# A fused memory-attention and mixture-of-experts kernel: splits of the first steps kept behind the prologue, some remainders on GpSimd, the last two token tiles one by one

## The chip, the cores and the metric

The kernel runs on one core of one Trainium2 chip. The metric is the device time of one execution in microseconds (us). The kernel before takes 1411.16 us, the median of three runs that lie between 1411.07 and 1411.36 us.

## The reference: what is computed

There are 8 batches with 8 heads, 576 tokens, head dimension 64, and 32 memory slots for each head. First comes an attention through the memory:

```python
a = softmax(phi, axis=2)                        # phi: (8, 8, 576, 32)
k_m = einsum('bhsm,bhsd->bhmd', a, k)           # 32 memory keys per head
v_m = einsum('bhsm,bhsd->bhmd', a, v)           # 32 memory values per head
attn = softmax(q @ k_m.T / sqrt(64))            # (8, 8, 576, 32)
x = (attn @ v_m) -> (4608 tokens, 512)
p = domain_probs / domain_probs.sum(-1)         # 4 experts
out = sum over e of p[:, e] * (relu(x @ w1[e]) @ w2[e])   # w1: 512x1024, w2: 1024x512
```

All of it is in 32-bit floats.

## The kernel before

**Two-part numbers.** TensorE multiplies in a rounded 32-bit form. To keep the precision, most operands are split in two: ScalarE casts the value to the rounded form (the high part), and another engine subtracts that from the value (the low part, here called the remainder). A product then takes three matmuls: high by high, high by low and low by high. `split` (L146 to L148) does this for weights: the cast is L147, the subtraction L148, on VectorE (DVE) or GpSimd (POOL) as its caller says.

**The work.** x is never formed. v_m is multiplied with w1 first (`vw_mm`, L458 to L463, and its two parts `vw_out`, L480 and L482), so that the first layer of an expert is one product of the transposed attention weights AT with that table vw. Two batches make a pair of 1152 tokens, nine token tiles of 128. A pair has 4 experts with 32 steps each (`first` and `second`); a step is one of the 8 blocks of 128 hidden units (j) for one half of one batch's tokens. `first(s)` makes h, the x product and its relu (matmuls L553 to L555, ScalarE L565, VectorE's remainder L567); `second(s)` multiplies two or three token tiles of h with w2 (L583 to L585) and sums over j in PSUM. `first` runs two steps ahead of `second`. When a half ends, `accumulate` (L603, L605) adds the probability-weighted sum into acc and, at the last expert, stores 256 KB per token tile from SyncE's queue (L607).

**Order.** The beginning (batch 0 up to the first two `first`) and everything from step 36 on stand in a `manual_schedule`: each engine runs them in the written order. Steps 0 to 35 are placed by the library's scheduler, which may move their instructions ahead, also into the gaps of the prologue. What a step does besides `first` and `second` is in a plan. Step 1 has, in this order: the scores of the last token group of batch 0, the splits of w1 for fh 1 (the upper half of the hidden units; four tiles), the splits of w2 for j = 2 to 5, v_m x w1 for hp 0 and 2 with fh 1, and batch 1's phi chain. Step 2 has the scores of the next token group and v_m x w1 for hp 1 and 3; step 5 has w2 for j = 6 and 7. Batch 1's keys and values follow at steps 6 to 10 (`unit_kv`, remainders on GpSimd, three buffers for the split parts), its v_m at 11. At steps 16 and 22 `v_split` casts v_m of batches 0 and 1 into two parts (vh), which two steps later are written to vs by 8 small DMAs for each batch. `phi_max` of batch 1 is already kept in program order.

**The prologue's middle.** For batch 0 the written order is: scores, `scores_max` (L401, L404), the split of w1 hp 1, the v_m tables of group 1 (`write_vt_0`, ScalarE L353 and VectorE L354), two further w1 splits with remainders on GpSimd, v_m x w1, `scores_exp` (L410), `vw_out` for hp 0, `soft` (L417 to L420), `vw_out` for hp 1 and 2, `transposes` (L441) and their copies AT (L452, L453), `vw_out` for hp 3, two w2 splits with remainders on GpSimd, `first(0)`, `first(1)`. `keep_warm` puts in products whose result isn't used.

**Loads.** All loads and stores go through SyncE's queue, in its order. Weights, keys and queries share four staging buffers of 512 KB; a load waits until the splits that read its buffer are done. The order of these loads is the order of the plan.

Of the kernel before, what the change touches and what calls it, by code (L numbers as in the profile page):

```python
# [40 lines left out]
N, DM, E, F = 4608, 512, 4, 1024  # L41
P = 128
# [4 lines left out]
NJ = F // P  # L47
TP = 2 * S // P
# [3 lines left out]
LAST = NG * PAIR  # L52
# [39 lines left out]
def body(ctx: ExitStack, tc: tile.TileContext, qm, qt, kv, kvt, phi, prob, w1, w1d, w2, out):  # L92
    nc = tc.nc
# [3 lines left out]
    psum = pool("psum", space=PSUM)  # L97
# [7 lines left out]
    pt = const.tile([P, N // P, E], F32, name="pt")  # L105
# [37 lines left out]

    w1t, w2t = {}, {}

    def split(dst, raw, eng):  # L146
        nc.scalar.copy(dst[:, 0, :], raw)  # L147
        eng.tensor_sub(dst[:, 1, :], raw, dst[:, 0, :].bitcast(F32))  # L148

    def split_w1(raw, fh, hp, eng):  # L150
        t = wp.tile([P, 2, 512], F32R, name="w1", tag="w1", bufs=4)
        split(t, raw[:, hp % 2, :], eng)
        w1t[fh, hp] = t

    def unit_w1(k, e, fh, g):
        def emit(raw):
            for i in range(2):
                split_w1(raw, fh, 2 * g + i, nc.vector)
        return ("w1", e, fh, g), emit

    def split_w2(k, e, j, raw, eng=nc.vector):
        t = wp.tile([P, 2, DM], F32R, name="w2", tag="w2", bufs=NJ + 1)
        split(t, raw[:, j % 2, :], eng)
        w2t[k, e, j] = t

    def units_w1(e, fh, g):
# [20 lines left out]
    st = {}  # L187
# [153 lines left out]
    def slot(b, h):  # L341
        return h ^ TURN[b % 4]

    def write_vt_0(b, gs=slice(0, 2)):

        vt = vts[b // 2].rearrange("p (g a) s c -> p g a s c", g=2)
        v = st["v", b].rearrange("p (g a) m -> p g a m", g=2)
        for h in range(4):
            q = slot(b, h)
            r = slice(64 * (h % 2), 64 * (h % 2) + 64)  # L350
            dst = vt[r, gs, h // 2, :, M * q:M * q + M]
            x = v[r, gs, q // 2, :]
            nc.scalar.copy(dst[:, :, 0, :], x)  # L353
            nc.vector.tensor_sub(dst[:, :, 1, :], x, dst[:, :, 0, :].bitcast(F32))  # L354

    def v_split(b):

        st["vh", b] = att.tile([P, 2, NP, M], F32R, name="vh", tag="vh")
        split(st["vh", b].rearrange("p s a m -> p s (a m)"),
              st["v", b].rearrange("p a m -> p (a m)"), nc.gpsimd)  # L360

    def write_v(b, pair):

# [170 lines left out]
    hs, mid, acc, po, ended = {}, {}, {}, {}, []  # L534

    def where(s):
        k, s = divmod(s, PAIR)
        e, s = divmod(s, STEPS)
        odd, s = divmod(s, 2 * NJ)
        half, j = divmod(s, NJ)  # L540
        return k, e, odd, half, j

    def first(s):
# [25 lines left out]
            )  # L569
        hs[s] = h  # L570

    def second(s):
        k, e, odd, half, j = where(s)
        h = hs.pop(s)
        w = w2t[k, e, j]
        t0 = (0, 2, 5, 7)[2 * odd + half]
        left = [(t0 + i, h[:, :, i * P:i * P + P]) for i in range(2)]
        if t0 == 5:
            left.append((4, mid[j]))
        for t, x in left:  # L580
            if j == 0:
                po[t] = psum.tile([P, DM], F32, name="p2", tag="p2", bufs=4)
            nc.tensor.matmul(po[t], x[:, 0, :], w[:, 0, :], start=j == 0, stop=False)  # L583
            nc.tensor.matmul(po[t], x[:, 0, :], w[:, 1, :], start=False, stop=False)  # L584
            nc.tensor.matmul(po[t], x[:, 1, :], w[:, 0, :], start=False, stop=j == NJ - 1)  # L585
        if j == NJ - 1:
            ended.append((k, e, t0, [t for t, _ in left]))

    def accumulate():
        if not ended:  # L590
            return
        k, e, t0, left = ended.pop()
        if e == 0:
            a = work.tile([P, 1024], F32, name="acc", tag="acc", bufs=4)
            for i in range(2):
                acc[k, t0 + i] = a[:, i * DM:i * DM + DM]
            if t0 == 5:
                acc[k, 4] = work.tile([P, DM], F32, name="accm", tag="accm", bufs=1)
        for t in left:
            a, n = acc[k, t], TP * k + t  # L600
            p = pt[:, n, e:e + 1]
            if e == 0:
                nc.vector.tensor_scalar_mul(a, po[t], p)  # L603
            else:
                nc.vector.scalar_tensor_tensor(a, po[t], p, a, ALU.mult, ALU.add)  # L605
            if e == E - 1:
                nc.sync.dma_start(out[n * P:n * P + P, :], a)  # L607


    plan = defaultdict(list)  # L610
# [15 lines left out]

    rest = [unit_scores(0, t0) for t0 in (2, 4)]
    rest += [lambda t0=t0: (transposes(0, t0), transposes_out(0, t0)) for t0 in (2, 4)]
    rest += [unit_w1(0, 0, 1, g) for g in range(2)]
    rest += [unit_w2(0, 0, j2) for j2 in range(1, 4)]  # L630
    rest += [lambda hp=hp: vw_unit(0, 0, 1, hp, (0,), ("pm", 4)) for hp in range(NP)]
    for s, u in zip(REST_0, rest):
        at(s, u)
# [120 lines left out]
    with tc.manual_schedule():  # L754
        raw = {key: take(later) for later, key in enumerate(early)}
        stage_ahead(len(early) + 4)
        nc.scalar.copy(att.tile([P, 1], F32, name="woken", tag="woken"), ident[:, :1])
        nc.sync.dma_start(pt, prob)
        keep_warm(10)
        dve, gps = nc.vector, nc.gpsimd  # L760
        for g in range(2):
            phi_max(0, g)
        for g in range(2):
            phi_exp(0, g)
        kvr = lambda hp: raw["kv", 0, hp]
# [24 lines left out]
        for hp in (2, 3):  # L790
            for c2 in range(2):
                kv_mm(0, hp, c2)
            kv_mm_tail(0, hp)
            if hp == 2:
                for i in range(2):
                    kv_fold(0, i)
        keep_warm(3)
        kv_pick(0, 0)
        w1g = [raw["w1", 0, 0, g] for g in range(2)]
        split_w1(w1g[0], 0, 0, gps)  # L800
        for hp in (2, 3):
            kv_out(0, hp)
        write_vt_0(0, slice(0, 1))
        q = raw["qm", 0, 0]
        scores_mm(0, 0, q, (0, 1))
        for hp in (2, 3):
            kv_fold(0, hp)
        keep_warm(5)
        kv_pick(0, 1)
        scores_mm(0, 0, q, (2, 3))  # L810
        scores_max(0, 0)
        split_w1(w1g[0], 0, 1, gps)
        write_vt_0(0, slice(1, 2))
        keep_warm(2)
        split_w1(w1g[1], 0, 2, gps)
        split_w1(w1g[1], 0, 3, gps)
        pv = [vw_mm(0, 0, hp, ("p2", 4)) for hp in range(4)]
        scores_exp(0, 0)
        vw_out(pv[0], 0, 0, 0, 0, (0,))
        soft(0, 0)  # L820
        keep_warm(3)
        for hp in (1, 2):
            vw_out(pv[hp], 0, 0, 0, hp, (0,))
        transposes(0, 0)
        keep_warm(4)
# [60 lines left out]
```

## Time and profile before

| what | value |
|---|---|
| median of three runs | 1411.16 us |
| the profiled execution's own time | 1411.33 us |
| its span, first to last instruction | 1409.6 us |
| TensorE busy | 1391.7 us (99%) |
| VectorE busy | 624.5 us (44%) |
| ScalarE busy | 579.6 us (41%) |
| GpSimd busy | 400.7 us (28%) |
| mean granted TensorE clock | 0.998 |

The page counts an engine as busy while it computes. PE is TensorE, DVE VectorE, ACT ScalarE, POOL GpSimd, and SPq the queue of SyncE, which issues DMAs. A group of rows names the line, the engine, the operation and the tiles (written from read). L12 is line 12 of the kernel before. Times in the rows count from the first instruction.

### The profile page before, as it was taken

How to read it: one execution, taken by the hardware profiler on the slowest of the kernel's cores; microseconds unless marked ns; L12 is line 12 of the kernel's file. 1: busy time of each engine (PE TensorE's matmuls, PEld its weight loads, DVE VectorE, ACT ScalarE, POOL GpSimd, SP SyncE). 2: the span in 40 equal slices, each digit the busy share in tenths (PEclk: the TensorE clock that was granted, in tenths of full speed). 3: DMA queues.
4: the chain of work that ended last, by engine and by line, in shares of the span. 5: the costliest groups of instructions: out<-in, count | busy, mean ns of one | idle time of the engine just before them, and what ended most of it. 6: DMA issues, size and time to landing. Idle time of an engine off the chain costs nothing.

```text
span 1409.6 us, 21662 instructions
## 1 busy us (share of the span) xinstructions
PE 1391.7 (99%) x7742; PEld 1217.9 (86%) x7742; DVE 624.5 (44%) x1470; ACT 579.6 (41%) x1536; POOL 400.7 (28%) x324
## 2 busy tenths in 40 slices
PE   7999999999999999999999999999999999999998
PEld 6888888888888888888888888888888888888887
DVE  7875535435553465344353445434343223222232
ACT  6755555433354456553353434435322312122221
POOL 4400354422234244441342424434220202020200
PEclk9999999999999999999999999999999999999999
DMA  6532332684232243333588675776742623233201
GB/s 251 184 96 75 123 98 91 231 253 128 76 130 95 71 143 109 111 98 105 138 299 243 234 257 173 277 216 224 240 123 64 176 67 105 76 105 76 60 31 38
DMA packets 74363, 200.47 MB, mean 142 GB/s; under 512 B 21904, under 2 KB 23056, under 8 KB 74256
## 3 DMA queue, kind: packets, MB, share of 16 engines
q1 hardware_dynamic: 74256, 199.09, 44.9%
q8 instruction: 62, 1.02, 0.3%
q14 instruction: 45, 0.37, 0.1%
HBM read 146.35 MB, written 51.38 MB: 140 GB/s over the span
## 4 chain that ended last, share of the span: by engine, by line
PE 93%; ACT 2%; DVE 2%; DMA 1%; issue 1%; SPq 0%; ACTq 0%
PE p L585 18%; PE p L583 18%; PE p L584 18%; PE p L553 10%; PE p L554 9%; PE p L555 9%; PE pv L506 3%; PE sc L391 2%; PE x L287 2%; PE pv L461 1%; PE pv L463 1%; PE pv L462 1%; DVE vw L482 1%; DMA stage<-in_w 1%; PE tp L441 1%
## 5 line engine op out<-in xcount | busy, mean ns | idle before, releaser
L148 POOL TENSOR_TENSOR w<-stage,w 128x512 fp32r<-128x512 f32 x230 | 297.2, 1293 | 719.4 <-ACT w L147 698.3
L567 DVE SCALAR_TENSOR_TENSOR h<-p,h 128x256 fp32r<-128x256 f32 x512 | 215.6, 421 | 443.3 <-ACT h L565 300.6
L585 PE MATMUL p<-w,h 128*128 128x512 f32 x1024 | 402.4, 393 | 0.9 <-DVE h L567 0.9
L583 PE MATMUL p<-w,h 128*128 128x512 f32 x1024 | 403.0, 394 | 0.0
L584 PE MATMUL p<-w,h 128*128 128x512 f32 x1024 | 402.3, 393 | 0.0
L565 ACT ACTIVATE h<-p 128x256 fp32r<-128x256 f32 x512 | 196.4, 384 | 484.8 <-PE p L555 465.5
L553 PE MATMUL p<-AT,vw 128*128 128x256 f32 (+1 forms) x1024 | 308.9, 302 | 2.3 <-DVE h L567 0.9
L554 PE MATMUL p<-AT,vw 128*128 128x256 f32 (+1 forms) x1024 | 302.7, 296 | 0.0
L555 PE MATMUL p<-AT,vw 128*128 128x256 f32 (+1 forms) x1024 | 301.5, 295 | 0.0
L585 PEld LDWEIGHTS p<-w,h 128*128 128x128 f32 x1024 | 192.5, 188 | 44.8 <-DVE h L567 1.4
L553 PEld LDWEIGHTS p<-AT,vw 128*128 128x128 f32 x1024 | 193.2, 189 | 22.6 <-DVE h L567 1.2
L583 PEld LDWEIGHTS p<-w,h 128*128 128x128 f32 x1024 | 192.4, 188 | 22.9
L584 PEld LDWEIGHTS p<-w,h 128*128 128x128 f32 x1024 | 192.5, 188 | 21.8
L554 PEld LDWEIGHTS p<-AT,vw 128*128 128x128 f32 x1024 | 193.8, 189 | 19.6
L555 PEld LDWEIGHTS p<-AT,vw 128*128 128x128 f32 x1024 | 192.8, 188 | 0.1
L147 ACT CAST w<-stage 128x512 fp32r<-128x512 f32 x264 | 161.9, 618 | 6.8 <-DMA stage<-in_w 4.6
L567 DVE SCALAR_TENSOR_TENSOR hm<-p,hm 128x64 fp32r<-128x64 f32 x256 | 56.1, 219 | 156.8 <-ACT h L565 155.7
L565 ACT ACTIVATE hm<-p 128x64 fp32r<-128x64 f32 x256 | 57.1, 223 | 161.5 <-PE p L555 161.5
L509 DVE TENSOR_TENSOR vst<-pv,vst 128x512 fp32r<-128x512 f32 x80 | 55.3, 692 | 113.2 <-ACT vst L508 112.9
L276 POOL TENSOR_TENSOR kvs<-stage,kvs 128x512 fp32r<-128x512 f32 x58 | 75.8, 1326 | 103.9 <-ACT kvs L275 103.5
L508 ACT CAST vst<-pv 128x512 fp32r<-128x512 f32 x80 | 46.9, 587 | 123.6 <-PE pv L506 123.6
L482 DVE TENSOR_TENSOR vw<-pv,vw 64x512 fp32r<-64x512 f32 x96 | 65.9, 688 | 24.7 <-ACT vw L480 23.5
(87 smaller groups left out, 1147.4 us busy)
## 6 DMA issues: line engine op xcount, KB each, us to landing
stage<-in_w SPq DMA_DIRECT2D x92, 512.0 KB, 4.2
vwd<-vst SPq DMA_DIRECT2D x80, 512.0 KB, 3.6
vw<-vwd SPq DMA_DIRECT2D x320, 128.0 KB, 3.8
stage<-in_w1d SPq DMA_DIRECT2D x40, 512.0 KB, 3.9
stage<-in_kv SPq DMA_DIRECT2D x32, 512.0 KB, 4.1
stage<-in_qm SPq DMA_DIRECT2D x16, 512.0 KB, 3.9
out<-acc SPq DMA_DIRECT2D x32, 256.0 KB, 2.1
ph<-in_phi SPq DMA_DIRECT2D x16, 288.0 KB, 4.4
```

The lines of the kernel that those rows point to most:

```text
L147: nc.scalar.copy(dst[:, 0, :], raw)
L148: eng.tensor_sub(dst[:, 1, :], raw, dst[:, 0, :].bitcast(F32))
L276: eng.tensor_sub(t[:, 1], src, t[:, 0].bitcast(F32))
L482: nc.vector.tensor_sub(t[r, 1, :], ps[r], t[r, 0, :].bitcast(F32))
L553: nc.tensor.matmul(ps, w[:, 0, f], at_t[:, g, 0, c], start=g == 0, stop=False)
L554: nc.tensor.matmul(ps, w[:, 0, f], at_t[:, g, 1, c], start=False, stop=False)
L555: nc.tensor.matmul(ps, w[:, 1, f], at_t[:, g, 0, c], start=False, stop=g == 1)
L565: nc.scalar.activation(t[:, 0, to], ps[:, at_], AF.Relu)
L567: nc.vector.scalar_tensor_tensor(t[:, 1, to], ps[:, at_], 0.0, t[:, 0, to].bitcast(F32), ALU.max, ALU.subtract)
L583: nc.tensor.matmul(po[t], x[:, 0, :], w[:, 0, :], start=j == 0, stop=False)
L584: nc.tensor.matmul(po[t], x[:, 0, :], w[:, 1, :], start=False, stop=False)
L585: nc.tensor.matmul(po[t], x[:, 1, :], w[:, 0, :], start=False, stop=j == NJ - 1)
```

## The change

`split` gets a flag `keep`. With it, the ScalarE cast is tied behind the ScalarE instruction that was written just before it (`tc.keep_in_program_order`). It is set for the splits of w1 for fh 1, of w2 for j = 2 to 7 (whose remainders go from VectorE to GpSimd), and for v_m of batches 0 and 1 (`v_split`). In the prologue the four v_m remainders of group 1 go from VectorE to GpSimd, and `vw_out` of hp 0 is written behind `soft` instead of before it. In the last two steps the token tiles are multiplied one after the other: at the last step but one only the first tile, at the last step the first tile's rest, its accumulation and store, then both steps of the second tile, which is accumulated and stored in two halves of 256 columns, the first from SyncE's queue, the second from ScalarE's.

```diff
-    def split(dst, raw, eng):
-        nc.scalar.copy(dst[:, 0, :], raw)
+    def split(dst, raw, eng, keep=False):
+        i = nc.scalar.copy(dst[:, 0, :], raw)
+        if keep:
+            tc.keep_in_program_order(i)
         eng.tensor_sub(dst[:, 1, :], raw, dst[:, 0, :].bitcast(F32))
...
         split(st["vh", b].rearrange("p s a m -> p s (a m)"),
-              st["v", b].rearrange("p a m -> p (a m)"), nc.gpsimd)
+              st["v", b].rearrange("p a m -> p (a m)"), nc.gpsimd, b < 2)
...
+        if s == LAST - 2:
+            multiply(k, e, t0, tile_of(hs[s], 0), j)
+            return
+        if s == LAST - 1:
+            multiply(k, e, t0, tile_of(hs[s], 0), j)
+            accumulate_tile(k, e, t0)
+            for i in (s - 1, s):
+                multiply(k, e, t0 + 1, tile_of(hs[i], 1), j - (s - i))
+            accumulate_tile(k, e, t0 + 1, 2)
+            return
...
+    def accumulate_tile(k, e, t, parts=1):
+        n = TP * k + t
+        p = pt[:, n, e:e + 1]
+        for i in range(parts):
+            c = slice(DM // parts * i, DM // parts * (i + 1))
+            a = acc[k, t][:, c]
...
             if e == E - 1:
-                nc.sync.dma_start(out[n * P:n * P + P, :], a)
+                (nc.scalar if i else nc.sync).dma_start(out[n * P:n * P + P, c], a)
...
-    rest += [unit_w1(0, 0, 1, g) for g in range(2)]
-    rest += [unit_w2(0, 0, j2) for j2 in range(1, 4)]
+    rest += [unit_w1(0, 0, 1, g, True) for g in range(2)]
+    rest += [unit_w2(0, 0, j2, nc.gpsimd, True) for j2 in range(1, 4)]
...
-        write_vt_0(0, slice(1, 2))
+        write_vt_0(0, slice(1, 2), gps)
...
         scores_exp(0, 0)
-        vw_out(pv[0], 0, 0, 0, 0, (0,))
         soft(0, 0)
         keep_warm(3)
-        for hp in (1, 2):
+        for hp in (0, 1, 2):
             vw_out(pv[hp], 0, 0, 0, hp, (0,))
```

## Rows read from the trace of the kernel before

**Rows 1.** Windows: length, engines' busy us (instructions), granted clock, DMA share, GB/s.
```profile
27.50:31.00 3.50, 0.75 (x7) 0.56 (x7) 3.44 (x8) 1.66 (x4) 0.46 (x1) 1.00 0.13 30
31.00:36.00 5.00, 5.00 (x31) 5.00 (x31) 4.92 (x6) 4.23 (x9) 2.49 (x2) 0.66 0.36 107
38.00:50.00 12.00, 12.00 (x75) 10.24 (x74) 11.67 (x31) 9.13 (x20) 5.14 (x4) 1.00 0.60 182
```

**Rows 2.** Waits of TensorE, 20 to 140 us: total, times, longest.
```profile
PE p L585 <- DVE h L567: 0.9, 1, 0.9
```

**Rows 3.** VectorE in order of time: start, us, line, operation, tiles, shapes.
```profile
24.24 2.43 DVE L354 TENSOR_TENSOR vt<-v,vt 64x32 fp32r<-64x32 f32 x4
26.70 0.69 DVE L148 TENSOR_TENSOR w<-stage,w 128x512 fp32r<-128x512 f32 x1
...
33.66 3.38 DVE L148 TENSOR_TENSOR w<-stage,w 128x512 fp32r<-128x512 f32 x2
...
42.24 0.67 DVE L482 TENSOR_TENSOR vw<-pv,vw 64x512 fp32r<-64x512 f32 x1
...
42.91 0.74 DVE L197 TENSOR_REDUCE nm<-ph 128x1 f32<-128x576 f32 x1
...
45.45 1.12 DVE L148 TENSOR_TENSOR w<-stage,w 128x512 fp32r<-128x512 f32 x1
...
89.02 0.68 DVE L453 TENSOR_TENSOR AT<-tp,AT 128x512 fp32r<-128x512 f32 x1
```

**Rows 4.** Groups of instructions: VectorE 20 to 62 us, GpSimd and ScalarE whole span.
```profile
L148 DVE TENSOR_TENSOR w<-stage,w 128x512 fp32r<-128x512 f32 x12 | 11.0, 932 | 0.7 <-ACT w L147 0.6
...
L148 POOL TENSOR_TENSOR w<-stage,w 128x512 fp32r<-128x512 f32 x230 | 297.2, 1293 | 719.4 <-ACT w L147 698.3 <-DVE hm L567 9.6 <-DMA vw<-vwd 8.8
L148 POOL TENSOR_TENSOR vh<-v,vh 128x128 fp32r<-128x128 f32 x8 | 3.7, 463 | 28.7 <-ACT vh L147 22.5 <-DVE vt L354 6.2
...
L147 ACT CAST w<-stage 128x512 fp32r<-128x512 f32 x264 | 161.9, 618 | 6.8 <-DMA stage<-in_w 4.6
```

**Rows 5.** GpSimd in order of time.
```profile
23.65 2.53 POOL L148 TENSOR_TENSOR w<-stage,w 128x512 fp32r<-128x512 f32 x2 [0.47 <-ACT w L147]
...
33.51 2.98 POOL L148 TENSOR_TENSOR w<-stage,w 128x512 fp32r<-128x512 f32 x2 [3.81 <-ACT w L147]
```

**Rows 6.** TensorE in order of time.
```profile
30.90 0.66 PE L441 MATMUL tp<-ident,at 128*128 128x128 f32 x4 [2.75 <-DVE at L420]
...
38.67 0.68 PE L391 MATMUL sc<-kT,stage 128*64 128x64 f32 x8
...
40.78 0.28 PE L553 MATMUL p<-AT,vw 128*128 128x256 f32 x1
...
42.85 1.89 PE L391 MATMUL sc<-kT,stage 128*128 128x64 f32 x16
...
56.51 1.18 PE L287 MATMUL x<-kvs,a 128*128 128x256 f32 x8
...
62.55 1.11 PE L287 MATMUL x<-kvs,a 128*128 128x256 f32 x8
...
89.49 0.31 PE L553 MATMUL p<-AT,vw 128*128 128x320 f32 x1
```

**Rows 7.** ScalarE in order of time.
```profile
41.46 0.42 ACT L410 ACTIVATE at<-at 64x256 f32<-64x256 f32 x1
```

**Rows 8.** SyncE's queue in order of time; loads 20 to 62 us with median to landing.
```profile
41.38 9.11 SPq L133 DMA_DIRECT2D stage<-in_kv  x4
...
stage<-in_qm SPq DMA_DIRECT2D x2, 512.0 KB, 3.6
```

**Rows 9.** The end, 1404 to 1410 us: order of time; DMA rate in 40 slices.
```profile
1404.67 1.43 DVE L605 SCALAR_TENSOR_TENSOR acc<-p,pt,acc 128x512 f32<-128x512 f32 x2 [2.58 <-PE p L585]
...
1405.45 1.01 SPq L607 DMA_DIRECT2D out<-acc  x2
...
GB/s 0 0 0 0 0 0 0 0 0 0 0 0 0 0 0 287 382 369 355 396 342 355 423 396 191 0 0 0 0 0 0 0 0 0 0 55 0 0 0 0
```

More of the change, by code (lines that the diff above doesn't have):

```diff
@@ L144, in body, with split_w1, unit_w1, split_w2 @@
     w1t, w2t = {}, {}
-    def split(dst, raw, eng):
-        nc.scalar.copy(dst[:, 0, :], raw)
+    def split(dst, raw, eng, keep=False):
+        i = nc.scalar.copy(dst[:, 0, :], raw)
+        if keep:
+            tc.keep_in_program_order(i)
         eng.tensor_sub(dst[:, 1, :], raw, dst[:, 0, :].bitcast(F32))
-    def split_w1(raw, fh, hp, eng):
+    def split_w1(raw, fh, hp, eng, keep=False):
         t = wp.tile([P, 2, 512], F32R, name="w1", tag="w1", bufs=4)
-        split(t, raw[:, hp % 2, :], eng)
+        split(t, raw[:, hp % 2, :], eng, keep)
         w1t[fh, hp] = t
-    def unit_w1(k, e, fh, g):
+    def unit_w1(k, e, fh, g, keep=False):
         def emit(raw):
             for i in range(2):
-                split_w1(raw, fh, 2 * g + i, nc.vector)
+                split_w1(raw, fh, 2 * g + i, nc.vector, keep)
         return ("w1", e, fh, g), emit
-    def split_w2(k, e, j, raw, eng=nc.vector):
+    def split_w2(k, e, j, raw, eng=nc.vector, keep=False):
         t = wp.tile([P, 2, DM], F32R, name="w2", tag="w2", bufs=NJ + 1)
-        split(t, raw[:, j % 2, :], eng)
+        split(t, raw[:, j % 2, :], eng, keep)
         w2t[k, e, j] = t
@@ L171, in units_w1, with unit_w2 @@
         return (("w1", e, fh, g), load), lambda: split_w1(kept[0], fh, 2 * g + 1, nc.gpsimd)
-    def unit_w2(k, e, j2):
+    def unit_w2(k, e, j2, eng=nc.vector, keep=False):
         def emit(raw):
             for i in range(2):
-                split_w2(k, e, 2 * j2 + i, raw)
+                split_w2(k, e, 2 * j2 + i, raw, eng, keep)
         return ("w2", e, j2), emit
@@ L342, in slot, with write_vt_0 @@
         return h ^ TURN[b % 4]
-    def write_vt_0(b, gs=slice(0, 2)):
+    def write_vt_0(b, gs=slice(0, 2), eng=nc.vector):
         vt = vts[b // 2].rearrange("p (g a) s c -> p g a s c", g=2)
@@ L353, in write_vt_0 @@
             nc.scalar.copy(dst[:, :, 0, :], x)
-            nc.vector.tensor_sub(dst[:, :, 1, :], x, dst[:, :, 0, :].bitcast(F32))
+            eng.tensor_sub(dst[:, :, 1, :], x, dst[:, :, 0, :].bitcast(F32))
     def v_split(b):
@@ L570, in first, with multiply @@
         hs[s] = h
+    def multiply(k, e, t, x, j):
+        w = w2t[k, e, j]
+        if j == 0:
+            po[t] = psum.tile([P, DM], F32, name="p2", tag="p2", bufs=4)
+        nc.tensor.matmul(po[t], x[:, 0, :], w[:, 0, :], start=j == 0, stop=False)
+        nc.tensor.matmul(po[t], x[:, 0, :], w[:, 1, :], start=False, stop=False)
+        nc.tensor.matmul(po[t], x[:, 1, :], w[:, 0, :], start=False, stop=j == NJ - 1)
     def second(s):
         k, e, odd, half, j = where(s)
+        t0 = (0, 2, 5, 7)[2 * odd + half]
+        tile_of = lambda h, i: h[:, :, i * P:i * P + P]
+        if s == LAST - 2:
[8 more added lines that the diff above has]
+            return
         h = hs.pop(s)
-        w = w2t[k, e, j]
-        t0 = (0, 2, 5, 7)[2 * odd + half]
-        left = [(t0 + i, h[:, :, i * P:i * P + P]) for i in range(2)]
+        left = [(t0 + i, tile_of(h, i)) for i in range(2)]
         if t0 == 5:
@@ L580, in second @@
         for t, x in left:
[L581 to L585, printed above, removed]
+            multiply(k, e, t, x, j)
         if j == NJ - 1:
@@ L599, in accumulate @@
         for t in left:
-            a, n = acc[k, t], TP * k + t
-            p = pt[:, n, e:e + 1]
+            accumulate_tile(k, e, t)
+    def accumulate_tile(k, e, t, parts=1):
[4 more added lines that the diff above has]
+            a = acc[k, t][:, c]
             if e == 0:
-                nc.vector.tensor_scalar_mul(a, po[t], p)
+                nc.vector.tensor_scalar_mul(a, po[t][:, c], p)
             else:
-                nc.vector.scalar_tensor_tensor(a, po[t], p, a, ALU.mult, ALU.add)
+                nc.vector.scalar_tensor_tensor(a, po[t][:, c], p, a, ALU.mult, ALU.add)
             if e == E - 1:
-                nc.sync.dma_start(out[n * P:n * P + P, :], a)
+                (nc.scalar if i else nc.sync).dma_start(out[n * P:n * P + P, c], a)
     plan = defaultdict(list)
```

## The prediction

> **What bounds the kernel now.** I read the windows first [rows 1], then the waits [rows 2], then each engine in order of time [rows 3, 5 to 8]. The reader should see in the windows that TensorE is busy without a hole from 38 to 50 us (12.00 of 12.00), and the page's first part gives it 99% of the whole span: behind the first 40 us a cheaper VectorE, ScalarE or GpSimd is worth nothing by itself. From 27.5 to 31 us TensorE works 0.75 of 3.50 us while VectorE works 3.44; from 31 to 36 it is busy, but at a granted clock of 0.66 in the mean (partly at 1.2 instead of 2.4 GHz), after that hole. What TensorE waited for: the transposes of group 0 stood 2.75 us behind the softmax's last VectorE operation [rows 6], and the first step's third product 0.9 us behind VectorE's remainder of h [rows 2].
>
> The order in time says what VectorE did meanwhile [rows 3]: three w1 remainders, the first at 26.70, between the softmax's operations, and two weight remainders of 3.38 us together from 33.66. They belong to steps 1 and later; the scheduler put them into the hand-ordered prologue because their data were there. So the change can win only in some 40 us at the head and 4 us at the tail.
>
> What can be lost before the last token group's scores start at 38.67 [rows 6]: 3.50 - 0.75 = 2.75 us idle, 5.00 x (1 - 0.66) = 1.70 us of clock, 0.9 us of wait: 5.35 us.
>
> **The head, step by step.** (a) *Splits pinned.* A pinned ScalarE cast goes behind the ScalarE instruction written before it, and its remainder waits for the cast. For w1 of fh 1 that instruction is the exp of the last token group (step 1), itself behind the prologue. Out of the softmax's way go those three remainders, 0.69 us each: 2.1 us. The four v_m remainders (2.43 us at 24.24) go to GpSimd, and vw_out of hp 0 (0.68, as every vw remainder) goes behind the softmax. What is late next: the exp can follow the scores' subtraction, which ends where the v_m remainders began, at 24.3, and takes about 0.6. The softmax behind it (a reduce and a product of the 0.7 that 512 elements take here, and 0.5 of small ones) ends at 26.8, or at 27.9 if its product loses most of a GpSimd instruction's length. Then the transposes no longer wait for VectorE but for TensorE itself: v_m x w1 and the warm-up products, which ended by 27.50 + 0.75 = 28.2 [rows 1]. So 28.2 instead of 30.90 [rows 6].
>
> *v_m remainders on GpSimd.* The trace shows no GpSimd operation of 64x32. Bounds: zero, and 0.46, the 128x128 one; I take 0.25, on the line through that row and the 1.29 of 128x512 [rows 4], so four in 1.0 us. They stand ahead of the w1 remainders of hp 2 and 3, which began at 23.65 and took 2.53 [rows 5]. GpSimd was idle for 0.47 before them, so they end some 0.6 later, at 26.8, and the last v_m x w1 product half a us behind that, at 27.4. At 0.46 each it is 28.2, and the transposes come at 29.0.
>
> Behind them VectorE does three vw remainders instead of two (0.68 each), then AT's: AT's low part is there at about 30.1 and the last vw remainder at 30.8. Four warm-up products run from 28.7 to 29.6 at full clock, since the hole that preceded the low clock is gone. The first three steps' x products are 3 x 0.7 us, the first step's h products 1.4 (from x at 40.78 to the next scores at 42.85 one of each took 2.07, rows 6), with 0.6 us of waiting for the two remainders: 29.6 + 2.1 + 1.4 + 0.6 = 33.7. VectorE's h remainder comes at 31.7, because the 3.38 us are gone, and the prologue's two w2 low parts, cast from 30.0 and 1.29 each on GpSimd, at 32 and 33.2. So scores of the last group start at 33.8 instead of 38.67: **-4.8 us**. That agrees with 5.35 less 0.6. Bounds: -5.2 and, with the late softmax, slow v_m and the low clock again (1.7), -2.5.
>
> (b) *What was hidden is now late.* The early splits gave w1 of fh 1 ahead of its use, so the v_m x w1 products behind the scores at 38.67 ran freely. Now the exp lags the scores by the old 2.8 us (38.67 to 41.46, rows 6 and 7), less one remainder of 0.69 that stood between: 35.9 to 36.6. Cast 0.62 and remainder 0.69 [rows 3, 4]: the first product at 37.2 to 37.9. TensorE has one step of x and h in between (2.07 behind the scores' 0.6): until 36.5. So 0.7 to 1.4 us idle, then a product of 0.7 (half a step's h products) per remainder of 0.69, with up to 1.1 us more where the last group's softmax interleaves. Eight pinned casts at 0.62 hold ScalarE from 36 to 41; the four vw casts follow and their remainders end at 44. TensorE fills this with steps 2 and 3. Their w2 low parts come from GpSimd: first cast at 39.2, then 1.29 each, 40.5 and 41.8, in time for products at 41 to 43.5. The six w2 remainders that leave VectorE are 5.9 us: twelve took 11.0 [rows 4], less four of w1 (2.1 and 1.69) and two at 56 us (1.3). VectorE was full from 38 to 50 (11.67 of 12), so they make room for the four w1 remainders there. The query tile of group 1 now loads only when w1's buffer is free, at 38.3, and lands 3.6 later [rows 8], at 42. I take **+1.6 us**, the middle of 0.7 and 2.5.
>
> (c) *Batch 1's chain.* Its phi maximum is kept behind hp 2's vw remainder: 42.24, then 42.91 [rows 3]. Both stay near 42.5, so this chain does not start earlier. Its inner delays do shrink: two w2 remainders, the first of 1.12 at 45.45, stood between its small VectorE operations. That is 2.2 us; and between its first two multiplications there is slack, 6.04 us from 56.51 to 62.55 [rows 6], where a cast and two GpSimd remainders need 0.62 + 2 x 1.29 = 3.2. It ends in AT's low part at 89.70 while TensorE starts that batch's first x product at 89.49 [rows 3, 6], so it must move up as much as TensorE does, 3.2 us. 2.2 plus 1 us of that slack does it: **0**. Bounds 0 and +3.2. On GpSimd six w2 remainders (7.7 us) join two tails and eight kv remainders; from 39 to 53 it is nearly full. The first kv tile, loaded at 41.38 [rows 8] when a w2 buffer fell free, loads at 44.4 and is split by 52.8; its product came at 56.51. So cover holds, with nothing to spare. The 16 small vs writes of batches 0 and 1 go behind steps 16 and 22 on SyncE; the loads that stood behind the early ones gain, and vs is not read before the pair's fourth expert.
>
> A rule bears on (b). In the rows two VectorE remainders take 3.38 us beside two of GpSimd at 2.98, where one alone takes 0.69 [rows 3, 5]. The Trainium skill ("SBUF — State Buffer", Who interferes with whom) says that a VectorE operation with two SBUF inputs and a GpSimd one that reads SBUF block one another for a whole instruction. By that rule moving w2 to GpSimd frees VectorE only while VectorE is not splitting as well; it is the second rival below.
>
> **The tail.** TensorE's products are the same 18; only their order differs. Before, two accumulations of 1.43 us together run from 1404.67, and two 256 KB stores follow from 1405.45 [rows 9]. Their data moves in ten slices of 0.15 us, from 1406.25, at some 350 GB/s, the second's right behind the first's. After, the first of the last two tiles is done 0.7 us earlier and its store is out of the way; the last tile's two halves end at 1405.8 and 1406.1 (half of 1.43 together, as one whole did). The last store starts when it did, but holds 128 KB less: 128 KB at 350 GB/s is 0.37. **-0.3 us**; bounds -0.6, and +0.5 if ScalarE's first DMA starts slowly (no row shows one).
>
> **Sum.** -4.8 + 1.6 + 0 - 0.3 = -3.5. The profiled execution took 1411.33 (1.73 around the span of 1409.6), 0.17 above the median of 1411.16. 1411.33 - 3.5 = 1407.8. The prologue bounds give 1411.33 - 5.2 + 0.7 - 0.6 = 1406.2 on one side.
>
> **Rivals.**
> 1. *Batch 1's chain sets the end of the head.* For: AT's last part is just in time in the old trace, and the chain's start is tied to the vw remainder. Against: the 2.2 us that leave it. If nothing is saved in it, (c) is +3.2 and the time is 1411.0; if half, 1409.4; between them 1410.2. Chance 0.17.
> 2. *GpSimd and VectorE block one another.* If the w1 remainders meet w2's on GpSimd, four cost 1.69 (half of 3.38) instead of 0.69: +4.0 on the way to fh 1, of which 1 us is filled by steps 2 and 3: +3.0, 1410.8. Against: w2's casts stand behind all w1 casts, so at most the last remainders meet. Chance 0.10.
> 3. *Slower.* TensorE is served in a fixed order. If the scheduler places the scores of token group 1, whose query tile now waits for w1's buffer, ahead of steps 2 and 3, TensorE stands from 36.5 until the tile lands. With w1's first pair split by 40 and 3.6 to land, it is 43.6: 7.1 us instead of 1.6, +5.5, and the low clock again, +1.7: 1407.8 + 7.2 = 1415.0. It decides from about 5 us of standing. For: the load is tied to that buffer. Against: those scores came at 42.85 in the old trace, behind two whole steps, and the load is no later than that here. Chance 0.09.
> 4. *The pins hold nothing:* the exp they hang on floats into the prologue and draws the splits along. Then only w2 and v_m on GpSimd help, about 1.2 us with the tail: 1410.1. Chance 0.06.
>
> **How the numbers follow.** Forecast 0.58, own range 1406.0 to 1409.0. What a measurement tells from no change is 0.2%, 2.8 us: 1408.3 and 1414.0. Of the forecast 0.52 lies below 1408.3, of rival 1, spread over 0 to +3.2, 0.03: faster 0.55. The rest of both (0.06 + 0.14), rivals 2 and 4 (0.16) and 0.02 of rival 3 are no change: 0.38. Slower 0.07. The range leaves rival 3 out and has 0.4 under the best corner, for what a relieved VectorE may save later: 1405.8 to 1411.2.
>
> **What would show it.** Right: the transposes start near 28.2; no clock below 1.00 from 28 to 36; no weight remainder on VectorE before the last group's exp; scores of that group near 33.8; 1 to 2 us of TensorE idle between 36 and 45, ahead of v_m x w1; the first x product of batch 1 near 86.3; the last store's data ending earlier by a third of a us. Wrong: a hole over 4 us between 36 and 45, batch 1's first x product no earlier than 89, or w1 remainders of 1.7 us on VectorE.

## The result and the profile after

The changed kernel takes 1414.64 us (median of 11 runs, 1414.07 to 1417.45); the kernel before takes 1411.16 (11 runs, 1410.30 to 1412.51). The ratio is 1.0026 (95% interval 1.0017 to 1.0035): 3.5 us **slower**, where 1407.8 was predicted. The profiled execution took 1417.45 us, with a span of 1415.7; it is the slowest of its eleven, so its sums come out some 3 us above the median.

Windows of the kernel after, to be laid beside [rows 1] (columns as there):

```profile
10.00:20.00 10.00, 8.41 (x49) 8.22 (x50) 7.71 (x14) 7.40 (x20) 5.35 (x5) 0.66 1.03 410
27.50:31.00 3.50, 3.09 (x22) 2.61 (x21) 3.37 (x7) 1.71 (x3) 0.41 (x1) 1.00 0.01 2
31.00:36.00 5.00, 4.36 (x31) 3.64 (x31) 3.44 (x9) 2.32 (x6) 2.54 (x2) 1.00 0.00 0
38.00:50.00 12.00, 10.75 (x61) 8.61 (x62) 9.12 (x20) 8.95 (x19) 6.88 (x5) 1.00 0.64 196
72.00:82.00 10.00, 8.16 (x45) 7.21 (x44) 4.89 (x19) 5.82 (x19) 0.00 (x0) 0.83 0.36 118
```

The hole in 27.5 to 31 us is gone (3.09 of 3.50 busy) and so is the low clock behind it. But 38 to 50 us, full before, now has 1.25 us idle, and a new hole with a low clock lies in 72 to 82. TensorE in order of time (start, us):

```profile
19.65 1.10 PE L393 MATMUL sc<-kT,stage 128*128 128x64 f32 x8 [0.32 <-ACT xs L300]
...
29.20 0.60 PE L443 MATMUL tp<-ident,at 128*128 128x128 f32 x4
...
35.50 0.68 PE L393 MATMUL sc<-kT,stage 128*64 128x64 f32 x8
...
57.03 1.10 PE L289 MATMUL x<-kvs,a 128*128 128x256 f32 x5
...
70.90 1.15 PE L289 MATMUL x<-kvs,a 128*128 128x256 f32 x8
...
74.52 0.51 PE L308 MATMUL kvp<-ident,xs 128*128 128x128 f32 x2 [1.84 <-ACT xs L300]
...
78.33 1.89 PE L393 MATMUL sc<-kT,stage 128*128 128x64 f32 x16
...
93.57 0.31 PE L555 MATMUL p<-AT,vw 128*128 128x320 f32 x1
```

The first scores start at 19.65 us here and at 18.69 before; the written order up to them is the same. Over all kernels below that start lies between 18.13 and 19.86, whatever the kernel, with a granted clock of 0.66 or 0.83 in 10 to 20 us. So every time of the head is told **from the first scores on**, which takes that chance out:

| from the first scores to | before | after |
|---|---|---|
| last group's scores of batch 0 | 19.98 | 15.85 |
| batch 1's first key product (L287, L289) | 37.82 | 37.38 |
| its fourth key product | 51.00 | 51.25 |
| batch 1's first scores | 55.55 | 58.68 |
| the accumulation at 164.77 us of before | 146.08 | 149.10 |

4.13 us are gained by the first line, and 0.44 are left at the second. TensorE's waits from 20 to 140 us, to be laid beside [rows 2]:

```profile
PE kvp L308 <- ACT xs L300: 1.8, 1, 1.8
PE pv L464 <- POOL w L150: 1.1, 2, 0.8
PE p L556 <- DVE AT L455: 0.8, 1, 0.8
PE p L579 <- POOL w L150: 0.7, 1, 0.7
PE p L578 <- ACT h L567: 0.7, 1, 0.7
PE x L289 <- POOL kvs L278: 0.5, 1, 0.5
...
```

The wait for the softmax and that for VectorE's remainder of h are gone; in their place are one of 1.8 us and several of up to 0.8 us each. VectorE in order of time, ScalarE behind it, and GpSimd:

```profile
65.05 2.38 DVE L150 TENSOR_TENSOR w<-stage,w 128x512 fp32r<-128x512 f32 x2
...
69.53 2.38 DVE L150 TENSOR_TENSOR w<-stage,w 128x512 fp32r<-128x512 f32 x2
71.84 0.14 DVE L202 TENSOR_SCALAR nm<-nm 128x1 f32<-128x1 f32 x1
...
1411.47 0.87 DVE L627 SCALAR_TENSOR_TENSOR acc<-p,pt,acc 128x256 f32<-128x256 f32 x2 [0.61 <-PE p L580]
```
```profile
37.44 4.25 ACT L147 CAST w<-stage 128x512 fp32r<-128x512 f32 x8
...
45.91 0.58 ACT L482 CAST vw<-pv 64x512 fp32r<-64x512 f32 x1 [2.98 <-PE pv L465]
46.52 0.78 ACT L208 ACTIVATE ph<-ph,nm 128x576 f32<-128x576 f32 x1
...
55.36 1.65 ACT L277 CAST kvs<-stage 128x512 fp32r<-128x512 f32 x3
...
72.01 0.78 ACT L208 ACTIVATE ph<-ph,nm 128x576 f32<-128x576 f32 x1 [1.72 <-DVE nm L202]
...
74.12 0.35 ACT L300 COPY xs<-x 128x256 f32<-128x256 f32 x1
```
```profile
40.20 1.93 POOL L150 TENSOR_TENSOR w<-stage,w 128x512 fp32r<-128x512 f32 x1 [5.92 <-ACT w L147]
...
52.86 2.55 POOL L150 TENSOR_TENSOR w<-stage,w 128x512 fp32r<-128x512 f32 x2 [1.55 <-issue]
56.05 5.01 POOL L278 TENSOR_TENSOR kvs<-stage,kvs 128x512 fp32r<-128x512 f32 x4 [0.64 <-ACT kvs L277]
```

And the kernel before: ScalarE, where batch 1's first phi exp stands ahead of two of the vw casts, and VectorE with the odd batch's first four w1 remainders:

```profile
43.87 0.78 ACT L206 ACTIVATE ph<-ph,nm 128x576 f32<-128x576 f32 x1 [0.18 <-DVE nm L200]
...
45.53 1.27 ACT L480 CAST vw<-pv 64x512 fp32r<-64x512 f32 x2 [0.79 <-PE pv L463]
46.82 0.62 ACT L275 CAST kvs<-stage 128x512 fp32r<-128x512 f32 x1
```
```profile
56.02 1.29 DVE L148 TENSOR_TENSOR w<-stage,w 128x512 fp32r<-128x512 f32 x2 [0.61 <-ACT w L147]
...
63.85 2.38 DVE L148 TENSOR_TENSOR w<-stage,w 128x512 fp32r<-128x512 f32 x2
```

The pinned casts run in one block from 37.44, as forecast. But ScalarE then holds batch 1's exp (46.52) behind a vw cast that stands 2.98 us for TensorE, and later its copy xs (74.12) behind batch 2's exp, which stands 1.72 us for VectorE. From 45.91 to 55.07 us ScalarE has no pause of more than 0.05 us, and the casts of batch 1's first key tile, whose load has landed at 50.18 us, come behind all that, at 55.36 (before: 46.82).

One loss lies outside the head. From 250 us on the distance to the kernel before grows by 0.10 to 0.16 us in nearly every expert, almost only in the half of 256 tokens of an even batch (its eight narrow steps take 17.43 instead of 17.29 us), and to 2 us in all. There, every engine has the same instructions in the same order as before. What differs is an address: with `vw_out` of hp 0 moved behind `soft`, the small tile z is allocated first, and the even batches' vw tables begin at byte 192096 of each partition instead of 191968.

### The profile page after: what moved, and what is told of

Its sections match the earlier page's. It is cut to its first block, busy times and chain, and to the rows that moved or that the text cites. A ratio compares the mean times of both kernels' runs of the same rounds, so it can differ in the third digit from the quotient of the medians.

```text
span 1415.7 us, 21674 instructions
## 1 busy us (share of the span) xinstructions
PE 1396.1 (99%) x7742; PEld 1218.1 (86%) x7742; DVE 618.6 (44%) x1461; ACT 579.3 (41%) x1536; POOL 409.7 (29%) x334
## 4 chain that ended last, share of the span: by engine, by line
PE 94%; ACT 2%; DVE 2%; DMA 1%; issue 1%; POOL 0%; SPq 0%; DVEq 0%; ACTq 0%
PE p L579 18%; PE p L580 18%; PE p L578 18%; PE p L555 10%; PE p L556 9%; PE p L557 9%; PE pv L508 3%; PE sc L393 2%; PE x L289 2%; PE pv L463 1%; PE pv L465 1%; PE pv L464 1%; PE tp L443 1%; DVE vw L484 1%; PE kvp L308 0%
## 5 line engine op out<-in xcount | busy, mean ns | idle before, releaser
L150 POOL TENSOR_TENSOR w<-stage,w 128x512 fp32r<-128x512 f32 x236 | 305.2, 1295 | 728.6 <-ACT w L147 704.8
```

## The experiments

Each kernel ran 11 times (f3 5, g1 7, g3 8, k3 10) beside 26 to 33 runs of the kernel before, whose median was 1411.28 to 1411.62. "Head" is the table's last line (before: 146.08). It comes from one trace of each kernel: before, e2, e4, h1, k1 and k2 have the same instructions in the same order up to there, and their heads lie between 145.41 and 146.08. So a difference of less than 0.7 us between two heads shows nothing.

**e1, address back.** The changed kernel, with one tile allocated earlier:

```diff
         scores_exp(0, 0)
+        vw_tile(0, 0, 0, 0, 0)
         soft(0, 0)
```


> The changed kernel with one line more: the first vw tile is allocated ahead of soft in the prologue, so that the four vw buffers of the even batch and z get back the addresses of the kernel before (191968 instead of 192096 in each partition). No instruction and no order differs. Theory A (the address): in the trace after, an even batch's narrow steps take about 2.106 instead of 2.09 us, which adds up to some 2.0 us from 250 us to the end; with the address back that goes: 1414.6 - 2.0 = 1412.6 us. Rival (the drift comes from the other rotation of PSUM banks, or from nothing that lies in the program): 1414.6, as after.

1413.30 us; ratio to before 1.0011 (1.0002 to 1.0020). In its trace the distance to before stays between 2.25 and 2.28 us from 165 to 1389 us: no drift. What is left is the head (147.52, +1.44; by the medians it is +1.8). **e2, address only**, is the kernel before with z allocated ahead of the first vw tile:

```diff
...
+        z = att.tile([P, 2 * H, 1], F32, name="z", tag="z", bufs=2)
         vw_out(pv[0], 0, 0, 0, 0, (0,))
-        soft(0, 0)
+        soft(0, 0, z)
```

> The kernel before with z allocated ahead of the first vw tile: the vw buffers of the even batch lie 128 bytes higher, as after the change, and nothing else differs. Theory A: 1411.2 + 2.0 = 1413.2 us, with the drift of 0.15 us for each expert in an even batch's narrow steps. Rival (PSUM banks or chance): 1411.2.

1413.84; ratio 1.0015 (1.0006 to 1.0023), 2.3 us slower without a changed instruction. VectorE's accumulations at the two ends of an odd and an even batch's narrow half, before and in e2:

```profile
1313.48 1.40 DVE L605 SCALAR_TENSOR_TENSOR acc<-p,pt,acc 128x512 f32<-128x512 f32 x2
...
1330.94 1.40 DVE L605 SCALAR_TENSOR_TENSOR acc<-p,pt,acc 128x512 f32<-128x512 f32 x2
...
1348.23 1.40 DVE L605 SCALAR_TENSOR_TENSOR acc<-p,pt,acc 128x512 f32<-128x512 f32 x2
```
```profile
1315.83 1.40 DVE L605 SCALAR_TENSOR_TENSOR acc<-p,pt,acc 128x512 f32<-128x512 f32 x2
...
1333.31 1.40 DVE L605 SCALAR_TENSOR_TENSOR acc<-p,pt,acc 128x512 f32<-128x512 f32 x2
...
1350.74 1.40 DVE L605 SCALAR_TENSOR_TENSOR acc<-p,pt,acc 128x512 f32<-128x512 f32 x2
```

Before: 17.46 and 17.29 us; e2: 17.48 and 17.43. The addresses of these tables and of z alone make the loss, 2.08 us between 62 us and the end (the distance to before grows from 0.43 to 2.51). And before, the odd half (17.46) already has the slow time: its tables begin at 151904, 96 above a multiple of 256, as the moved ones do.

**h1, both tables moved** (before, e2's edit, and an unused tile ahead of the odd batch's buffers):

```diff
+        att.tile([P, 32], F32, name="pad", tag="pad")
         kvr = lambda hp: raw["kv", 0, hp]
```


> The kernel before with other addresses alone: 128 unused bytes ahead of the odd batch's vw buffers (152032 instead of 151904, so 224 instead of 96 above a multiple of 256) and z ahead of the even batch's (192224 instead of 191968: 224 above a multiple of 256, as before). Theory A2 (the place of a vw table within 256 bytes sets the narrow steps' time; before, only the odd batch's tables lie at 96, and its narrow half takes 17.46 us where the even batch's takes 17.29, as the even batch's does at 96 in e2: 17.43): the odd narrow half falls to 17.29 in each of 16 rounds, 16 x 0.17 = 2.7 us, time 1408.7. Rival (the odd half's 0.17 us have another reason, or the place within 512 bytes decides, by which the even batch gets worse): 1411.3, or up to 1413.5.

1409.24; ratio 0.9985 (0.9976 to 0.9994), 2.1 us **faster** than the kernel before with its instructions unchanged. The odd narrow half now takes 17.32 us, the even one 17.29:

```profile
1310.94 1.40 DVE L605 SCALAR_TENSOR_TENSOR acc<-p,pt,acc 128x512 f32<-128x512 f32 x2
...
1328.26 1.40 DVE L605 SCALAR_TENSOR_TENSOR acc<-p,pt,acc 128x512 f32<-128x512 f32 x2
...
1345.55 1.40 DVE L605 SCALAR_TENSOR_TENSOR acc<-p,pt,acc 128x512 f32<-128x512 f32 x2
```

**k1 and k2** are h1 with other pads:

```diff
-        att.tile([P, 32], F32, name="pad", tag="pad")
+        att.tile([P, 48], F32, name="pad", tag="pad")   # k2: 16
```


> As h1 (the kernel before with both kinds of vw tables moved; 1409.2 us), with 192 unused bytes instead of 128, so that all nine tables begin 32 above a multiple of 256. If 224 is the one good place of the four that the 64-byte grid allows (96 costs 0.16 us per narrow half): 1409.2 + 2 x 2 = 1413.5 us. Rival (96 is the one bad place): 1409.2.

> As k1 with 64 unused bytes: the tables begin 160 above a multiple of 256. If 224 alone is good: 1413.5 us; if 96 alone is bad: 1409.2; if 32 is as 224 and 160 as 96, the place within 128 bytes doesn't matter and this is 1413.5 while k1 is 1409.2.

k1: 1410.90 (0.9982 to 0.9999); k2: 1408.57 (0.9970 to 0.9988). Neither "only 224 is good" nor "only 96 is bad" holds; the narrow halves have four lengths:

| tables begin, above a multiple of 256 | narrow half, odd / even (us) | odd batch's wide half |
|---|---|---|
| 96 (before's odd, e2's even) | 17.46 / 17.43 | 22.37 |
| 32 (k1) | 17.38 / 17.34 | 22.47 |
| 224 (h1) | 17.32 / 17.29 | 22.35 |
| 160 (k2) | 17.27 / 17.25 | 22.33 |

The pad moves the tiles behind it as well, so in h1, k1 and k2 the vw tables aren't proved to be the cause; in e1 and e2 only the even batch's tables and z move. Nor is 160 shown to be better than 224: the intervals of k2 and h1 overlap, and the five halves of 320 tokens of an even batch that took 21.94 us before, and in h1, take 22.04 us in k2.

**e4, tail only**: the kernel before with the change's `multiply`, `second` and `accumulate_tile`, and nothing else of it.

> The kernel before with the change's tail alone (last two token tiles one by one, last store in two halves on two queues). As predicted: -0.3 us, 1410.9, since the last store holds 128 KB less. Rival: the last store's fixed time decides, not its bytes; from the start of the last matmul to the end of the span the traces have 4.67 us before and 4.65 after: 1411.2.

1411.35 against 1411.51, ratio 0.9997 (0.9988 to 1.0006): not to be told from nothing. From the last matmul's start to the end of the span it is 4.63 us in both traces. The two halves of the accumulation end 0.91 us behind that matmul's end, the whole one 0.79; the last store's data still land earlier, 3.10 instead of 3.25 us behind the matmul's start. But SyncE then goes through four semaphore waits instead of two, and the 0.15 us are gone.

**The head.** Up to g3, all of these have the old addresses (e1's line).

**e3, w2 on VectorE**:

```diff
-    rest += [unit_w2(0, 0, j2, nc.gpsimd, True) for j2 in range(1, 4)]
+    rest += [unit_w2(0, 0, j2, nc.vector, True) for j2 in range(1, 4)]
```

> As e1, and the six w2 remainders of the first steps go back to VectorE (their casts stay in program order). Theory B (GpSimd, filled with them from 40 to 62 us, holds the staging buffers, so that batch 1's keys and odd w1 arrive late): the odd batch's w1 loads come some 4 us earlier than 58.6, batch 1's first x product near 90 instead of 93.6, and the time is 2 to 3 us under e1: about 1410. Rival (VectorE then delays the w1 remainders and the softmaxes by as much, 5.9 us of work in a stretch where it is 9.1 of 12 busy): the time of e1, with TensorE waiting for VectorE's remainders between 36 and 50 us.

1413.44, as e1; head 147.55 (e1 147.52). The odd w1 load comes no earlier (39.6 us from the first scores, e1 39.0), and the first key product later (39.02, e1 37.46), though the first key load is issued 2.4 us earlier (23.8, e1 26.2). Theory B falls: six remainders taken off GpSimd win nothing, and TensorE waits for VectorE's vw (0.6) and h (0.4) instead.

**f1, no pins**, and **f4, pins on w1 only**, which has the last two of these edits:

```diff
-    rest += [unit_w1(0, 0, 1, g, True) for g in range(2)]
+    rest += [unit_w1(0, 0, 1, g) for g in range(2)]
...
-    rest += [unit_w2(0, 0, j2, nc.gpsimd, True) for j2 in range(1, 4)]
+    rest += [unit_w2(0, 0, j2, nc.gpsimd) for j2 in range(1, 4)]
...
-              st["v", b].rearrange("p a m -> p (a m)"), nc.gpsimd, b < 2)
+              st["v", b].rearrange("p a m -> p (a m)"), nc.gpsimd)
```

> As e1 (changed kernel with the old addresses, 1413.3 us), without the program order for any of the splits: w1, w2 and v_m casts are free again, the GpSimd remainders, the later vw_out and the tail stay. Theory C (the program order ties eight casts behind the last group's exp at 37 us, so that TensorE's work up to batch 1's first product takes 21.6 instead of 17.8 us): that stretch shrinks by 2 us or more, the transposes come about 1.4 us later (two w1 remainders beside the softmax), and the time is 1410.5 to 1412. Rival D (GpSimd's new load does the harm, not the order): 1413.3 or more, with the odd w1 loads still near 58.5 us.

> As e1, with the program order kept for w1 alone; w2 and v_m splits are free. Theory C in part: w2's casts fill ScalarE's time between 30 and 37 us, GpSimd does w2 there instead of in 40 to 46 and 53 to 55 us, the staging buffers come free some 4 us earlier and batch 1's chain with them: 1411 to 1412. Rival (w1 behind the exp is the late item): 1413.3, with the stretch to batch 1's first key product still at 21 us.

f1: 1412.33 (0.9996 to 1.0014), head 146.88; the last group's scores are back at 18.56 (before 19.98). f4: 1412.02 (0.9997 to 1.0015), head 146.20, scores at 15.86. The pins of w1 bring the gain at 16 us. The pins of w2 and v_m cost 1.3 us by the heads of e1 and f4; the intervals of the two times overlap. They do not cost it in the way that f4's forecast says: its first key load comes 3.6 us earlier than e1's, as forecast, but its first key product later (38.01).

**f2, w1 ahead**: step 1's w1 units are written ahead of its scores, so that their casts hang on a relu at 34.3 us and not on the exp.

```diff
-    for s, u in zip(REST_0, rest):
+    pairs = list(zip(REST_0, rest))
+    for i in (4, 5):
+        at(*pairs[i])
+    for s, u in pairs[:4] + pairs[6:]:
         at(s, u)
```


> As e1, with the two w1 units of step 1 written ahead of that step's scores, so that their casts are tied behind the relu of step 2 instead of the last group's exp. Theory C: the casts fill ScalarE's empty 34.5 to 37 us, the first product of v_m and w1 starts near 36 instead of 37.9, and the time is 1.5 to 2.5 us lower: 1411 to 1412. Rival (batch 1's own chain of phi, ScalarE and GpSimd sets the end of the head, whatever TensorE has done before): the first product of batch 1's keys stays near 57.0 and the time at 1413.3.

1411.42, ratio 0.9999 (0.9990 to 1.0009): by the medians 1.9 us better than e1, though the two intervals overlap. ScalarE and TensorE in order of time:

```profile
34.59 2.17 ACT L147 CAST w<-stage 128x512 fp32r<-128x512 f32 x4
...
42.13 0.78 ACT L208 ACTIVATE ph<-ph,nm 128x576 f32<-128x576 f32 x1 [0.31 <-DVE nm L202]
```
```profile
54.44 0.36 PE L289 MATMUL x<-kvs,a 128*128 128x256 f32 x1
...
72.08 0.44 PE L308 MATMUL kvp<-ident,xs 128*128 128x128 f32 x2 [1.84 <-ACT xs L300]
...
75.04 2.79 PE L393 MATMUL sc<-kT,stage 128*128 128x64 f32 x16
```

From the first scores (19.75): batch 1's exp at 22.4 (after: 26.9, before: 25.2), its first key product at 34.69 (37.38, 37.82). The chain now starts its products 3.1 us earlier than before, nearly the 3.2 that the forecast asked of it. But 0.9 of that is lost by the fourth key product (48.76, before 51.00), and the hole ahead of the last key transposes (1.84) takes back most of the rest, with a slow clock behind it (2.79 us for scores that take 1.89).

**f3, batch 2's phi kept** (e1; its maximum and exp in program order). **g4, odd w1 kept** (e1; the odd batch's four w1 units). **g2** is f2 with the same.

```diff
...
-        if b == 1:                  # f3, phi_max; phi_exp(2) is kept likewise
+        if b in (1, 2):
...
-            at(W1_1[2 * fh + g], unit_w1(0, 0, fh, g))        # g4, g2
+            at(W1_1[2 * fh + g], unit_w1(0, 0, fh, g, True))
```

> As e1, with batch 2's phi maximum and exp kept in program order, too (they are written at steps 25 and 26 and float ahead otherwise). Theory E (TensorE's 1.8 us before batch 1's last key transposes at 74.4 us stand because ScalarE does batch 2's phi exp, 1.7 us late behind w1 remainders on VectorE, ahead of the copy xs): the copy comes right behind its product and the time is 1.2 to 1.8 us lower: 1411.5 to 1412.1. Rival (another late item is right behind it): 1413.3.

> As e1 (old addresses, the change otherwise as it is; 1413.3 us), and the odd batch's four w1 casts kept in program order. Theory E alone: the stretch from batch 1's last key product to its first scores shrinks from 5.8 to 4.5 us, and the time by 1.2 us or more: 1411.5 to 1412.1. Rival (as f3: the next late item stands there): 1413.3.

> As f2, and the odd batch's four w1 casts are kept in program order, which puts them behind the copies xs of batch 1 on ScalarE, and their remainders off VectorE's queue ahead of batch 2's phi. Theory E (in f2 the last key transposes stand 1.8 us for the copy xs behind late w1 work, and f3 only swapped one late item for the next): no wait for xs over 0.6 us, batch 1's first scores at 53 us behind the first scores instead of 55.3, time 1.5 to 2.3 us under f2: 1409.1 to 1409.9. Rival (the w1 tables of the odd batch then come too late): no gain, with TensorE's waits on w1 between 76 and 95 us: 1411.4 or more.

f3: 1417.95, head 150.05, worse by 4.7 us than e1. TensorE and ScalarE show the next late item in the same place, an odd w1 cast that waits for its load:

```profile
67.78 0.44 PE L310 MATMUL kvp<-ident,xs 128*128 128x128 f32 x2 [2.33 <-ACT xs L302]
```
```profile
66.32 0.62 ACT L147 CAST w<-stage 128x512 fp32r<-128x512 f32 x1 [2.38 <-DMA stage<-in_w]
```

g4: 1413.78, head 148.65: a miss, with batch 1's scores at 57.03 (e1 57.10). Its wait for xs is gone, but the last key product now waits 0.96 us for a remainder on GpSimd, whose cast stands behind batch 2's exp. g2: 1411.24 (0.9991 to 1.0008), head 145.78; the hole is gone, batch 1's scores come at 54.08 (53 was expected), but its last transposes at 89.73 (before 89.86), behind a softmax (1.38 us of wait). **g1** (f2 with w2 and v_m free) and **g3** (g1 with g2):

> As f2 (old addresses, w1 splits written ahead of step 1's scores; 1411.4 us), and the w2 and v_m splits free as in f4. Theory C (late splits hold staging buffers and ScalarE, and batch 1's chain with them): batch 1's first key product comes some 34 us behind the first scores, as in f2 (34.7; before 37.8), and the loads behind it 2 us earlier, so that the time is 1.0 to 1.5 us under f2: 1410 to 1410.4. Rival (the two gains are the same one): 1411.4.

> g1 and g2 together. Theories C and E: their gains add where they lie in different stretches; 1408.5 to 1409.5, faster than the kernel before by 0.15% or more. Rival (batch 1's later chain, scores to attention weights, takes back what comes earlier): not under 1410.5.

1413.45 and 1415.04, heads 147.37 and 147.56: misses; the gains of f2 and f4 do not add, the first key product is at 39.72 and 38.61.

**h3 and h6** are g2 with h1's addresses; in h6 only the lower half's odd w1 is kept. **k3** is h6 with the last two w2 remainders on VectorE.

```diff
+            at(W1_1[2 * fh + g], unit_w1(0, 0, fh, g, fh == 0))      # h6
...
+    rest += [unit_w2(0, 0, j2, nc.gpsimd if j2 < 3 else nc.vector, True) for j2 in range(1, 4)]   # k3
```

> g2 (w1 ahead of the scores, odd w1 kept; 1411.2 us) with the addresses of h1. Theory A2: 1411.2 - 2.7 = 1408.5 us. Rival: 1411.2.

> As h3, but of the odd batch's w1 only the four splits for the lower half of the hidden units are kept in program order, so that those of the upper half don't come late (in g2 the odd batch's first scores come 1.5 us earlier than before, but its last transposes only 0.1). Theory E: the last transposes of the odd batch come 88.5 instead of 89.7 us behind the first scores, 1 us under h3: 1407.5. Rival (the tables of the lower half are what is late): as h3, 1408.5.

> As h6 (the fastest so far, 1408.5 us), with the two last w2 remainders of the first steps (j = 6 and 7), which stand right ahead of batch 1's key remainders on GpSimd, back on VectorE; TensorE's order is the same. Step (c) of the prediction (GpSimd has nothing to spare there): TensorE's 1.7 us of waiting for the key remainders fall under 0.7, the second key product comes 1 us earlier than 41.5 us behind the first scores, and the time is up to 1 us lower: 1407.5. Rival (the softmax that then waits for VectorE ahead of the last transposes takes it back): 1408.5.

h3: 1408.83 (0.9975 to 0.9993). h6: 1408.51 (0.9971 to 0.9989). k3: 1408.23 (0.9969 to 0.9988), the lowest of all, 3.4 us under the kernel before; the larger part of that is the addresses (h1: 2.1), and its head is 144.90. That k3 is faster than h6 is not shown: the intervals overlap. Its step did not come true either: TensorE's waits for key remainders fell from 1.7 to 0.8 us, but the second key product did not come earlier (41.57; h6 41.46). Where the two traces part is how late batch 2's phi landed, 1.4 us apart when counted from the first scores; h6 first:

```profile
63.40 0.75 DVE L199 TENSOR_REDUCE nm<-ph 128x1 f32<-128x576 f32 x1 [2.43 <-DMA ph<-in_phi]
```
```profile
62.77 0.75 DVE L199 TENSOR_REDUCE nm<-ph 128x1 f32<-128x576 f32 x1 [0.90 <-DMA ph<-in_phi]
```

(From the first scores 45.27 and 43.85, though the load was issued at 39.20 and 39.33.)

## Why the prediction was wrong

The loss adds up: head +1.44 (e1's trace), addresses +2.08 (e2's), tail 0.00 (e4's), together +3.5, as measured. That it fits to a tenth is luck: by the medians e1 and e2 lose 1.8 and 2.3 us, and one trace's head is good to 0.7. Against the forecast of -3.5 some 7 us were missed: 0.65 in (a), 2.2 in (b), 1.8 in (c), 2.1 by the addresses and 0.3 at the tail. The first x product of batch 1 came at 93.57 us, where the prediction named 86.3 as right and 89 as wrong.

- **(a) held.** Transposes at 9.55 from the first scores, before 12.21; no clock under 1.00 from 27.5 to 36 us; no weight remainder on VectorE ahead of the last exp; that group's scores 4.13 us earlier (-4.8 was said). TensorE waited 0.8 us for AT's low part, 0.2 more than the 0.6 allowed for all waits there.
- **(b) was too small, +1.6 for +3.7.** From those scores to batch 1's first key product TensorE has the same 112 matmuls in both kernels, and they took 21.53 instead of 17.84 us. Its largest waits there are w2's first low part from GpSimd (0.7) and a relu (0.7). f2 shows where most of it comes from: with the w1 casts 2.95 us earlier the stretch is 18.85 long.
- **(c) failed**: "Its inner delays do shrink", hence 0. From batch 1's first key product to the end of the head e1 loses 1.8 us: 0.7 up to the fourth key product and 1.2 at the copy xs, less 0.1 behind it. I followed that chain on VectorE, where it did as said (phi's maximum at 43.26 us in e1, 42.4 if that kernel had started as before; the forecast was 42.5). I didn't look at what is queued ahead of it on ScalarE. The scheduler put a vw cast there that waits for TensorE, so the exp came 1.7 us later than before; the first kv tile, forecast to be "split by 52.8", got its casts from 55.36 on and its last remainder at 58.6; and the copy xs stood behind batch 2's exp. Shown by a run of its own is the last of these: with f2's order and the odd w1 casts kept, the wait for xs goes (g2). What the late exp costs by itself is not shown: in f2 it comes 2.8 us earlier than before, and TensorE still loses 3.4 us from the first key product to the end of the head.
- GpSimd, on which (c) was made to rest ("nothing to spare"), was not what held the chain: e3 and k3 took w2 off it and the key products did not come earlier. Behind the last group's scores its own lateness is small in the kernel after: 0.7 us at w2's first low part, 0.5 us at a key remainder.
- **Rival 1** (batch 1's chain sets the end of the head) is what happened, beyond its own limit: it was priced up to "nothing is saved in it", +3.2, and the head came out 1.4 us longer than before. f2 shows it best: TensorE reaches the first key product 3.1 us earlier than before, and the head is no shorter (146.38). **Rival 2** met w2 once: GpSimd's first w2 remainder ran beside VectorE's last w1 remainder and took 1.93 us instead of 1.29, and TensorE's wait of 0.7 us for w2's low part ends with it. It met the odd batch's w1, too: before, one pair of remainders took 1.29 us with GpSimd idle (56.02) and one 2.38 beside its key remainders (63.85); now both pairs run beside them, later, and take 2.38 each. The Trainium skill ("SBUF — State Buffer", Who interferes with whom) has these two operations block one another; the trace agrees, with 2.38 against 1.29 us. The second pair (69.53) stands right ahead of batch 2's phi on VectorE (71.84), and so holds its exp and the copy xs. **Rivals 3 and 4** did not occur.
- **The addresses** were in no step, and at +2.1 us they cost more than the head. The sum took everything between the first 40 us and the last 4 as unchanged because no instruction changes there.
- **The tail**: 0.00 for -0.3, inside the bounds. The two halves take longer than one whole, so the last store starts later, and the program's end doesn't follow the 0.15 us that are left (e4).

What stays open: why 4 us gained at 16 us never pass batch 1's softmax. In g2, h3 and h6 the waits behind it moved to the last transposes (1.3 to 1.4 us). Only k3's head (144.90) lies below those of the kernels with the old head, and the landing of a load had a part in it.

## What to carry to other kernels

When work is moved up or tied down, follow the next chain through every in-order queue that it passes, and ask for each of its instructions which one now stands ahead of it and what that one waits for; an engine that is half idle can still be the one that holds it. Compare the tile addresses of the two programs as well as the instructions: a small tile that was allocated one line earlier shifted four tables by 128 bytes, and this cost 2.1 us, more than the head's 1.4. Measure the head from a first event that both kernels share, since the start alone moved by 1.7 us.

## What the runs showed of the hardware

- With the place of the vw tables changes the pace of the narrow steps: 17.25 to 17.46 us for eight, by the table above, with the same instructions. For the even batch's tables at 96 and 224, e1 and e2 show it with nothing else moved but z. The odd batch's wide half hardly changes between 96, 224 and 160 (22.33 to 22.37). Which access pays for it isn't settled: the loss is 0.018 us in a step of 2.09, spread over products that records of 0.01 us don't separate.
- The same hole of 1.8 us ahead of the key transposes was followed by a granted clock of 0.77 over 70.9 to 78.3 us in the profiled run of after, and by 1.00 in e1's; with it, the stretch took 7.43 instead of 5.78 us. The windows of after and of e1:

```profile
70.90:78.30 7.40, 5.56 (x26) 4.81 (x25) 4.23 (x18) 4.85 (x17) 0.46 (x1) 0.77 0.47 165
```
```profile
70.90:76.60 5.70, 3.92 (x26) 3.41 (x25) 2.73 (x12) 4.22 (x14) 0.30 (x1) 1.00 0.59 209
```

- In e4 the last store's data land 0.15 us earlier behind the last matmul than before, and the program still ends 4.63 us behind that matmul's start.
